# Second attention of a fused attention and MLP kernel: six more exps summed by VectorE, two new instruction orders, and batch 2's statistics moved behind it

## The chip, the cores and the metric

One core of one Trainium2 chip runs the whole program. The time is the device time of one execution in microseconds, the median of several runs. TensorE (PE in the profile) multiplies matrices, VectorE (DVE), ScalarE (ACT) and GpSimd (POOL) work on elements, and SyncE (SP) issues most of the transfers. The engines run side by side, each through its own queue in order, and wait for each other by semaphores. The matmul memory PSUM is used here as eight banks of 512 float32 columns.

## The reference

Attention with normalised queries and keys, then a two-layer MLP:

```python
q_n, k_n = rmsnorm(q, g_q), rmsnorm(k, g_k)        # x / sqrt(mean(x * x) + 1e-6) * g
attn = softmax(q_n @ k_n.T / 8)                    # 8 batches, 12 heads, 448 x 448
x = concat_heads(attn @ v)                         # 3584 x 768
out = gelu_tanh(x @ w_in) @ w_out                  # 768 -> 2048 -> 768
```

Inputs and output are float32; the matmuls run in bfloat16.

## The kernel before, in words

The batches are worked one after another, and two stages overlap. `attention(b)` does the attention of batch b and, in its gaps, the second MLP layer of the batch before. Behind it stands the first MLP layer of batch b, in whose time the operands of batch b + 1 are prepared. The attention of batch 0 has its own code; "the second attention" is that of batch 1.

**The twelve heads** go in three groups of four, called c = 0, 1, 2; group 1 holds "the middle heads". A group has seven units. A unit (line 335) is four 64x64 matmuls of scores into a pair of PSUM banks; ScalarE takes the exp of it (line 343) into SBUF. When a group's seven exps are there, TensorE sums them for the softmax (word `s`) and multiplies them with v (word `x`), both in `products` (line 387), which issues four matmuls for each operand in its list `es`. To shorten the sum, VectorE can add exps beforehand: step A adds exps 0, 1 to 2, 3 (line 355), B adds 4, 5 (line 358), F folds the two halves into one (line 360), G adds exp 6 (line 362). `added(b, c)` says how many are added; in the second attention it gives 6, 0 and 5 for the three groups. After the sum come T (two transposes, line 397), R (reciprocal, line 402), S (spread, line 409), and M (line 422), which writes `xT`, the input of the first layer.

**The order** of the attention is written out by hand. In `SECOND` (line 577) the first string is TensorE's order (`5r` is five steps of four matmuls of the second layer, line 495; `u` a unit), the second is VectorE's, and the third says before which exp ScalarE copies a finished tile of the second layer out. Words such as `J0`, `K0`, `L0`, `a0` in VectorE's string are places for further work, given to them in a list `extra`.

**PSUM** is four pairs of banks in a ring (`rounds`); `pair(...)` takes the one that was taken longest ago. The second layer holds one during the attention. In the first layer, `mm1_turn(b, i, ...)` works on the i-th of eight pairs of tiles, in turns: the first three pairs begin with the first two thirds of the sum ("early") before the loop over f, since the last `xT` isn't there yet. At f = 1 and f = 3 the "late" thirds of pairs 0 and 1 follow, at f = 5 that of pair 2, which also opens pair 3. When a pair is complete, ScalarE applies the Gelu (line 543).

**The preparation of batch 2:** for each group, squares of q and k (line 164 on GpSimd, line 162 on ScalarE), their totals over 64 columns (line 173, VectorE), a root, the product with the root (line 278, GpSimd), a transpose by DMA (line 319, SyncE), and for k a gain (line 325, VectorE). Groups 0 and 1 have their squares and totals at the places J0 to a5 of the second attention and their roots from ScalarE's Ln and Exp at its end. Group 2's squares follow at the end of the attention; its totals and its root by Newton's method (`rsqrt_last`, lines 254 to 262, 14 VectorE instructions) are issued at f = 0 of batch 1's first layer. Newton keeps two of its operands in PSUM, in a pair of their own from `pair("root")`.

Of the kernel before, what the change touches and what calls it, by code (L numbers as in the profile page):

```python
# [17 lines left out]
def kernel(  # L18
# [11 lines left out]
    nc = tc.nc  # L30
    B, H, S, D = q.shape
# [38 lines left out]
    def pair(name):  # L70
        rounds.append(rounds.pop(0))
        return rounds[-1]
# [65 lines left out]
    def late_loads(b, c):  # L138

        for n in "qk":  # L140
            for go in load(b, c, n):
                nc.vector.memset(raws[n, b, c][:1, 0, 0, :1], 0.0)
                go()
# [13 lines left out]
    def square(b, c, n, eng, hs=both, ts=slice(0, NT)):  # L157
        if (n, b, c) not in sqs:
            sqs[n, b, c] = sqp.tile([P, 2, NT, D], F32, tag="sq", name="sq")
        sq, raw = squares(b, c, n, hs, ts), raws[n, b, c][:, hs, ts]  # L160
        if eng is nc.scalar:
            nc.scalar.activation(sq, raw, AF.Square)  # L162
        else:
            eng.tensor_mul(sq, raw, raw)  # L164
# [5 lines left out]
    def total(b, c, n, hs=both, ts=slice(0, NT)):  # L170
        if b not in sss:
            sss[b] = smp.tile([P, NCH, 2, 2, NT], F32, tag="ss", name="ss")
        nc.vector.reduce_sum(  # L173
            sss[b][:, seat(b, c), "qk".index(n), hs, ts], squares(b, c, n, hs, ts), axis=AX.X
        )
# [6 lines left out]
    def place(b, c):  # L182
        if (b, c) == (0, NCH - 1):
            t = ps_m.tile([128, 512], F32, tag="mm", name="root")[:, :4 * NT]
        else:
            i = c % 2 * 4 * NT
            t = oall[1][:, S + i:S + i + 4 * NT]
        roots["qk", b, c] = t.rearrange("p (n a t) -> p n a t", n=2, a=2)
        for n in range(2):
            roots.setdefault(("qk"[n], b, c), roots["qk", b, c][:, n])  # L190
        return t
# [48 lines left out]
                dst, t[:, js], 1.5, y[:, js], op0=ALU.add, op1=ALU.mult  # L240
            )

    def rsqrt_last(b):


        c, flat, m = slice(NCH - 1, NCH), "p c n a t -> p (c n a t)", 4 * NT
        y, ms = rinvs[b][:, c].rearrange(flat), sss[b][:, c].rearrange(flat)
        if steady():
            own, dst = pair("root")[:, 0], y
        else:  # L250
            own, dst = oall[0][:, S:], place(b, 1)
        z, u = own[:, :m], own[:, m:2 * m]
        t = smp.tile([P, NCH * 4 * NT], F32, tag="lg", name="lg")[:, :m]
        nc.vector.tensor_scalar(u, ms, 1.0 / D, 1e-6, op0=ALU.mult, op1=ALU.add)
        nc.vector.tensor_scalar(
            y.bitcast(I32), u.bitcast(I32), -0.5, float(0x5F3759DF), op0=ALU.mult, op1=ALU.add
        )
        for i in range(3):
            nc.vector.tensor_copy(z, y)
            nc.vector.tensor_mul(t, z, y)  # L260
            nc.vector.scalar_tensor_tensor(z, t, -0.5, u, op0=ALU.mult, op1=ALU.mult)
            nc.vector.scalar_tensor_tensor(
                y if i < 2 else dst, z, 1.5, y, op0=ALU.add, op1=ALU.mult
            )
# [81 lines left out]

    def added(b, c):

        return NT - 1 if b > 1 else (NT - 1, 0, NT - 2)[c] if b else 0

    def add_exps(b, c, step):
        ex = exs[b, c]
# [18 lines left out]
    def products(b, c, what, lo=0, hi=NT):  # L371

        if lo == 0 and steady():
            o = oas["o", c, what] = pair("o")
            oas[what] = oas[c, what] = [o[:, r, :S] for r in range(2)]
        elif lo == 0:
            oas[what] = spare.pop() if spare else [o[:, :S] for o in oall]
        o = oas[what]
        es = [exs[b, c][:, t] for t in range(NT)]
        if not what and added(b, c):  # L380
            es[:added(b, c) + 1] = [ess[b, c][:, 0]]
        n = len(es)
        for i in range(lo, min(hi, n)):
            for r in range(2):
                rs = slice(r * R, (r + 1) * R)
                for a in range(2):
                    nc.tensor.matmul(  # L387
                        o[r][a * D:(a + 1) * D],
                        vb[b % 2][rs, 2 * c + a, i] if what else ones[rs], es[i][rs, a],
                        start=(i == 0), stop=(i == n - 1),  # L390
                    )
# [156 lines left out]
    def mm1_pair(i, cs=range(HP), b=0, js=range(2)):  # L548
# [27 lines left out]
    )  # L576
    SECOND = (
        "3r u 5r uu 8r u 8r uu 8r u 5r u 4r u 7r us 4r u 4r u 3r uu 4r x 1r usu 3r u 6r u 2r u 5r"
        " uu 10r x 6r sx",
        "A0 L0 B0 F0 G0 J0 T0 R0 K0 S0 a0 a1 M0 T1 R1 S1 a2 A2 a3 B2 F2 M1 a4 a5 T2 R2 S2 M2",  # L580
        {6: 0, 14: 1, 21: 2},
    )

    def attention(b, side, extra, ends):
# [65 lines left out]
        for word in order.split():  # L650
            if word.endswith("r"):
                for _ in range(int(word[:-1])):
                    next(m2)
                    go_on()
                continue
            for w in word:
                k = n[w]
                n[w] += 1
                if w == "u":
                    for fn in side.get(k, ()):  # L660
                        fn()
                    unit(b, *units[k])
                    made.add(("unit", k))
                else:
                    last = added(b, k)
                    assert {("u", t) for t in range(k * NT, (k + 1) * NT)} <= made
                    assert w == "x" or not last or ("FG"[last - NT + 2], k) in made
                    products(b, k, "sx".index(w))
                    made.add((w, k))
                go_on()  # L670
# [254 lines left out]
    for b in range(B):  # L925
        m1, side, extra, ends = [], [], [], []
        if b == 0:

            m1 = [(0, lambda: total(1, 0, "k"),
                   lambda: total(1, 2, "q"), lambda: total(1, 2, "k"),  # L930
                   lambda: rsqrt_newton(1), lambda: normed_both(1, 2, nc.gpsimd),
                   lambda: normed(1, 0, "k", nc.gpsimd)),
                  (2, lambda: total(1, 1, "q"), lambda: total(1, 1, "k"),
                   lambda: normed(1, 0, "q", nc.vector), lambda: rsqrt_last(1),
                   lambda: normed_both(1, 1, nc.vector)),
                  (6, lambda: trans(1, 0, nc.scalar)),
                  (7, lambda: trans(1, 1))]
            extra += [("first", lambda: late_loads(2, 0)), ("L0", lambda: late_transposed(1, 2)),
                      ("L0", lambda: late_loads(2, 1)), ("a1", lambda: late_loads(2, 2)),
                      ("K0", lambda: gain(1, 2))]  # L940

            for n in "qk":
                sqs[n, 2, 1] = [
                    nrmp.tile([P, NT, 2, D], BF16, tag=f"nrm{m}", name="sq")
                    .rearrange("p t a d -> p (t a d)").bitcast(F32)
                    .rearrange("p (a t d) -> p a t d", a=1, t=NT) for m in "qk"
                ]

            extra += [("J0", lambda: gpsimd_waits(ess[1, 0][:1, 0, 0, :1])),
                      ("K0", lambda: gpsimd_waits(kT[:1, 2, 0, 0, :1]))]  # L950
            at = 0
            for c in range(2):
                for n in "qk":
                    for hs in (slice(0, 1), slice(1, 2)) if c else (both,):
                        extra += [
                            ("K0" if at else "J0",
                             lambda c=c, n=n, hs=hs: square(2, c, n, nc.gpsimd, hs)),
                            (f"a{at}", lambda c=c, n=n, hs=hs: total(2, c, n, hs))]
                        at += 1
        elif b + 1 < B:  # L960

            m1.append((0, lambda: gpsimd_waits(ess[b, NCH - 1][:1, 0, 0, :1])))
            for c in range(NCH):
                if b == 1 and c + 1 == NCH:
                    m1 += [(0, lambda: total(2, 2, "q")), (0, lambda: total(2, 2, "k")),
                           (0, lambda: rsqrt_last(2))]
                m1 += [(0, lambda c=c: normed_both(b + 1, c, nc.gpsimd)),
                       (4 * c + 4, lambda c=c: transposed(b + 1, c))]
            m1 += [(9, lambda: gain(b + 1, 0)), (14, lambda: gain(b + 1, 1))]
        if 0 < b and b + 2 < B:  # L970
            m1 += [(4, lambda: loads(b + 2, 1)), (8, lambda: loads(b + 2, 2))]
            for c, at in ((0, 4), (1, 9)):
# [38 lines left out]
            break  # L1011
        nc.scalar.preload_act_table_set(EXP_SET)
        if b + 2 < B:
            ends.append(lambda: rsqrt(b + 2, slice(0, NCH if b else NCH - 1)))
            side += [(0 if b else 11, lambda: load_v(b + 2, 0, HP))]
            if b + 3 < B:
                side.append((3, lambda: loads(b + 3, 0)) if b else (14, lambda: late_loads(3, 0)))
# [38 lines left out]
```

## Time and profile before

| what | us |
|---|---|
| median of 3 runs (391.13 to 391.48) | 391.18 |
| the profiled execution | 391.23 |
| its span, first to last instruction | 389.2 |
| second attention, TensorE's part | 50.07 to 75.93 |
| first layer of batch 1 | 75.93 to 94.54 |
| third attention | 94.54 to 121.38 |

Line numbers (L387) are those of the kernel before. In a view by groups, the figures behind the bar are the busy time and the mean of one instruction in ns, then the engine's idle time before the group and what ended it. In a timeline a row is its start, its length, the engine, the line, the operation, output and inputs, and how often it stands there in a row; a bracket gives the idle time ahead of it. In the chain of work that ended last, a row is the start, the length, the engine, the tile and the line. The table of windows gives each engine's busy time, the granted clock of TensorE, the share of the transfer engines and their GB/s. The ends of matmuls are modelled, so their starts are read.

### The profile page before, as it was taken

How to read it: one execution, taken by the hardware profiler on the slowest of the kernel's cores; microseconds unless marked ns; L12 is line 12 of the kernel's file. 1: busy time of each engine (PE TensorE's matmuls, PEld its weight loads, DVE VectorE, ACT ScalarE, POOL GpSimd, SP SyncE). 2: the span in 40 equal slices, each digit the busy share in tenths (PEclk: the TensorE clock that was granted, in tenths of full speed). 3: DMA queues.
4: the chain of work that ended last, by engine and by line, in shares of the span. 5: the costliest groups of instructions: out<-in, count | busy, mean ns of one | idle time of the engine just before them, and what ended most of it. 6: DMA issues, size and time to landing. Idle time of an engine off the chain costs nothing.

```text
span 389.2 us, 17542 instructions
## 1 busy us (share of the span) xinstructions
PE 380.6 (98%) x8060; PEld 294.0 (76%) x8060; DVE 235.9 (61%) x366; ACT 278.7 (72%) x353; POOL 126.3 (32%) x110
## 2 busy tenths in 40 slices
PE   7899999999999999999999999999999999999996
PEld 4565577877887788877888788877888778887664
DVE  5998938976596359836589257953598204980010
ACT  6995499767994689757995589946897449944300
POOL 5996506384005440093103740064300900000000
PEclk9999999999999999999999999999999999999999
DMA  8999999999614992379822995159631721120033
GB/s 266 322 231 211 210 230 263 223 200 264 113 44 100 243 213 58 80 132 217 194 65 65 214 227 103 45 110 251 108 80 50 125 44 42 44 65 4 2 83 81
DMA packets 64446, 54.68 MB, mean 141 GB/s; under 512 B 37620, under 2 KB 60020, under 8 KB 64372
## 3 DMA queue, kind: packets, MB, share of 16 engines
q1 hardware_dynamic: 53936, 41.33, 43.8%
q0 software_dynamic: 10128, 11.80, 18.5%
q8 instruction: 63, 1.03, 1.1%
q10 hardware_dynamic: 308, 0.43, 0.4%
q14 instruction: 11, 0.09, 0.1%
HBM read 45.61 MB, written 11.01 MB: 146 GB/s over the span
## 4 chain that ended last, share of the span: by engine, by line
PE 92%; ACT 5%; DMA 1%; issue 1%; DVE 0%; POOL 0%; DVEq 0%
PE t L537 33%; PE t L495 32%; PE t L387 9%; PE t L335 7%; PE t L463 5%; ACT ex L343 4%; PE t L556 4%; DMA rawq<-in_q_dram 1%; PE h L436 1%; PE tp L296 1%; PE o L387 0%; POOL nrmq L278 0%; ACT g L543 0%; DVE ss L173 0%; ACT sq L162 0%
## 5 line engine op out<-in xcount | busy, mean ns | idle before, releaser
L343 ACT ACTIVATE ex<-t,shift 128x896 bf16<-128x896 f32 x168 | 156.2, 1016 | 1.9 <-PE t L335 1.6
L495 PE MATMUL t<-wout,g 64*64 64x384 bf16 (+1 forms) x3456 | 150.6, 305 | 0.0
L537 PE MATMUL t<-xT,win 64*64 64x448 bf16 x2688 | 128.7, 349 | 0.3 <-ACT g L543 0.3
L495 PEld LDWEIGHTS <-g 64*64 64x64 bf16 x3456 | 112.9, 107 | 19.2
L537 PEld LDWEIGHTS <-win 64*64 64x64 bf16 x2688 | 96.6, 107 | 31.0 <-issue 0.5
L543 ACT ACTIVATE g<-t 128x896 bf16<-128x896 f32 x56 | 50.5, 915 | 57.1 <-PE t L537 57.1
L173 DVE TENSOR_REDUCE ss<-sq 128x14 f32<-128x896 f32 (+3 forms) x45 | 44.5, 997 | 51.9 <-ACT sq L162 49.1
L335 PE MATMUL t<-qT,kT 64*64 64x448 bf16 x672 | 58.2, 351 | 1.4 <-ACT ex L343 0.6
L799 POOL COPY mark<-es 1x1 bf16<-1x1 bf16 x7 | 1.2, 177 | 132.0 <-DVE es L362 128.3
L355 DVE TENSOR_TENSOR es<-ex 128x1792 bf16<-128x1792 bf16 x20 | 21.2, 1061 | 33.0 <-ACT ex L343 33.0
L278 POOL TENSOR_TENSOR nrmq<-rawq,rinv 128x896 bf16<-128x896 f32 (+1 forms) x21 | 34.9, 1660 | 18.6 <-ACT rinv L205 11.0
L278 POOL TENSOR_TENSOR nrmk<-rawk,rinv 128x896 bf16<-128x896 f32 (+1 forms) x21 | 34.4, 1640 | 0.0
L387 PE MATMUL t<-ex,vb 64*64 64x448 bf16 x588 | 31.9, 350 | 0.0
L335 PEld LDWEIGHTS <-kT 64*64 64x64 bf16 x672 | 25.5, 106 | 7.3 <-DVE kT L305 1.2
L397 DVE STREAM_TRANSPOSE st<-t 128x448 f32<-128x448 f32 x42 | 24.7, 626 | 9.7 <-PE t L387 9.7
L387 PEld LDWEIGHTS <-vb 64*64 64x64 bf16 x672 | 23.5, 107 | 7.3 <-issue 1.0
L409 DVE STREAM_TRANSPOSE rb<-rc 128x896 f32<-128x896 f32 (+1 forms) x25 | 26.7, 1068 | 0.3
L705 DVE COPY osb<-t 128x384 f32<-128x384 f32 (+1 forms) x4 | 2.0, 507 | 35.2 <-PE t L463 35.2
L422 DVE TENSOR_TENSOR xT<-t,rb 128x896 bf16<-128x896 f32 x21 | 22.8, 1087 | 0.8
L164 POOL TENSOR_TENSOR sq<-rawq 128x896 f32<-128x896 f32 (+1 forms) x9 | 13.6, 1513 | 28.6 <-DVE ss L173 27.3
L513 ACT COPY osb<-t 128x768 f32<-128x768 f32 (+1 forms) x18 | 12.6, 701 | 13.9 <-PE t L495 13.9
L358 DVE TENSOR_TENSOR es<-es,ex 128x1792 bf16<-128x1792 bf16 x20 | 21.3, 1063 | 0.7 <-ACT ex L343 0.6
(103 smaller groups left out, 313.5 us busy)
## 6 DMA issues: line engine op xcount, KB each, us to landing
rawq<-in_q_dram SPq DMA_DIRECT2D x22, 448.0 KB, 5.0
rawk<-in_k_dram SPq DMA_DIRECT2D x22, 448.0 KB, 5.8
out_dram<-osb SPq DMA_DIRECT2D x42, 192.0 KB, 2.7
vb<-in_v_dram POOLq DMA_DIRECT2D x6, 672.0 KB, 7.3
win<-in_moe_w_in_dram POOLq DMA_DIRECT2D x8, 384.0 KB, 10.8
wout<-in_moe_w_out_dram POOLq DMA_DIRECT2D x3, 768.0 KB, 17.1
out_dram<-osb SPq DMA_DIRECT2D x24, 96.0 KB, 3.7
vb<-in_v_dram POOLq DMA_DIRECT2D x2, 448.0 KB, 15.5
```

Source lines behind the costliest of these rows:

```text
L173: nc.vector.reduce_sum(sss[b][:, seat(b, c), "qk".index(n), hs, ts], squares(b, c, n, hs, ts), axis=AX.X)
L278: eng.tensor_mul(nrms[n, b, c][:, ts].rearrange("p t a d -> p a t d"), raws[n, b, c][:, :, ts], root[:, :, ts].to_broadcast([P, 2, m, D]),)
L335: nc.tensor.matmul(sc[r * R:(r + 1) * R, a, :S], kT[rs, c, t, r], qT[b][rs, c, :, r], start=True, stop=True,)
L343: nc.scalar.activation(exs[b, c][:, t], scs.pop((b, c, t))[:, :, :S], AF.Exp, scale=scale, bias=shift)
L358: nc.vector.tensor_add(es, es, ex[:, 4:6])
L387: nc.tensor.matmul(o[r][a * D:(a + 1) * D], vb[b % 2][rs, 2 * c + a, i] if what else ones[rs], es[i][rs, a], start=(i == 0), stop=(i == n ...
L397: nc.vector.transpose(st[:, r].rearrange("p a b -> p (a b)"), o[r])
L409: nc.vector.transpose(oas["rb"][:, rs].rearrange("p r s -> p (r s)"), rc.to_broadcast([128, (rs.stop - rs.start) * m, 32]),)
L422: nc.vector.tensor_mul(xT[b][:, 2 * c:2 * c + 2], oas["o", c, 1][:, :, :S], oas["rb"])
L495: mm = nc.tensor.matmul(o[a * R:(a + 1) * R, bank, :hi - lo], g[rs, f, at:at + R], wout[rs, f, lo:hi], start=(n == 0), stop=(n == len(step ...
L537: mm = nc.tensor.matmul(h[a * R:(a + 1) * R, j, :S], win[rs, c, at:at + R], xT[b][rs, c], start=begin and c == cs[0], stop=end and c == cs ...
L543: nc.scalar.activation(g[:, 2 * i:2 * i + 2, (b % 2) * S:(b % 2 + 1) * S], h[:, :, :S], AF.Gelu_apprx_tanh,)
```

## The change

1. `added(1, 1)` becomes 5: the middle heads' exps 0 to 5 are added by steps A and B. F isn't done for them: `products` takes the two added halves and exp 6, three operands instead of seven.
2. `SECOND` gets a new order for TensorE and for VectorE and other places for ScalarE's copies. Only two places a0 and a1 are left for totals, those of group 0.
3. Batch 2's group 1: the four half squares on GpSimd and the four half totals on VectorE go to f = 0 of batch 1's first layer, ahead of the totals of group 2. Its root leaves ScalarE's Ln and Exp and joins Newton, which now works on 56 columns and comes before all of GpSimd's products of batch 2 in the program.
4. Newton's two PSUM operands no longer take a pair of their own. They lie in columns 448 on of the two banks of the pair taken last, `rounds[-1]`.
5. The gain of batch 2's group 1 moves from f = 14 to the start of the third attention; the loads of batch 2's group 2 are issued at a0 instead of a1.

```diff
-    def rsqrt_last(b):
+    def rsqrt_last(b, c=slice(NCH - 1, NCH)):
...
         if steady():
-            own, dst = pair("root")[:, 0], y
+            z, u = (rounds[-1][:, i, S:S + m] for i in range(2))
+            dst = y
...
-        return NT - 1 if b > 1 else (NT - 1, 0, NT - 2)[c] if b else 0
+        return NT - 1 if b > 1 else (NT - 1, NT - 2, NT - 2)[c] if b else 0
...
-            es[:added(b, c) + 1] = [ess[b, c][:, 0]]
+            es[:added(b, c) + 1] = [ess[b, c][:, i] for i in range(1 + ((b, c) == (1, 1)))]
...
-        "3r u 5r uu 8r u 8r uu 8r u 5r u 4r u 7r us 4r u 4r u 3r uu 4r x 1r usu 3r u 6r u 2r u 5r"
-        " uu 10r x 6r sx",
-        "A0 L0 B0 F0 G0 J0 T0 R0 K0 S0 a0 a1 M0 T1 R1 S1 a2 A2 a3 B2 F2 M1 a4 a5 T2 R2 S2 M2",
-        {6: 0, 14: 1, 21: 2},
+        "7r u 1r uu 9r u 7r u 1r u 1r u 9r u 10r u 3r u 1r s 3r u 4r u 1r u 7r ux 2r u 3r u 4r us"
+        " 2r u 5r uu 4r u 2r x 10r sx",
+        "A0 L0 B0 F0 G0 J0 T0 R0 K0 A1 S0 B1 M0 a0 T1 R1 A2 S1 B2 F2 M1 a1 T2 R2 S2 M2",
+        {8: 0, 13: 1, 21: 2},
...
+            if b == 1:
+                halves = [(n, slice(a, a + 1)) for n in "qk" for a in range(2)]
+                m1 += [(0, lambda n=n, hs=hs: square(2, 1, n, nc.gpsimd, hs)) for n, hs in halves]
+                m1 += [(0, lambda n=n, hs=hs: total(2, 1, n, hs)) for n, hs in halves]
+                m1 += [(0, lambda n=n: total(2, 2, n)) for n in "qk"]
+                m1.append((0, lambda: rsqrt_last(2, slice(1, NCH))))
             for c in range(NCH):
-                if b == 1 and c + 1 == NCH:
-                    m1 += [(0, lambda: total(2, 2, "q")), (0, lambda: total(2, 2, "k")),
-                           (0, lambda: rsqrt_last(2))]
                 m1 += [(0, lambda c=c: normed_both(b + 1, c, nc.gpsimd)),
                        (4 * c + 4, lambda c=c: transposed(b + 1, c))]
...
-            ends.append(lambda: rsqrt(b + 2, slice(0, NCH if b else NCH - 1)))
+            ends.append(lambda: rsqrt(b + 2, slice(0, NCH if b else 1)))
```

More of the change, by code (lines that the diff above doesn't have):

```diff
@@ L241, in rsqrt_newton @@
             )
-    def rsqrt_last(b):
-        c, flat, m = slice(NCH - 1, NCH), "p c n a t -> p (c n a t)", 4 * NT
+    def rsqrt_last(b, c=slice(NCH - 1, NCH)):
+        flat, m = "p c n a t -> p (c n a t)", (c.stop - c.start) * 4 * NT
         y, ms = rinvs[b][:, c].rearrange(flat), sss[b][:, c].rearrange(flat)
         if steady():
-            own, dst = pair("root")[:, 0], y
-        else:
-            own, dst = oall[0][:, S:], place(b, 1)
-        z, u = own[:, :m], own[:, m:2 * m]
+            z, u = (rounds[-1][:, i, S:S + m] for i in range(2))
+            dst = y
+        else:
+            z, u = oall[0][:, S:S + m], oall[0][:, S + m:S + 2 * m]
+            dst = place(b, 1)
         t = smp.tile([P, NCH * 4 * NT], F32, tag="lg", name="lg")[:, :m]
@@ L666, in attention @@
                     assert {("u", t) for t in range(k * NT, (k + 1) * NT)} <= made
-                    assert w == "x" or not last or ("FG"[last - NT + 2], k) in made
+                    assert w == "x" or not last or ("BG" if (b, k) == (1, 1) else "FG")[
+                        last - NT + 2] + str(k) in {x + str(i) for x, i in made}
                     products(b, k, "sx".index(w))
@@ L938 @@
             extra += [("first", lambda: late_loads(2, 0)), ("L0", lambda: late_transposed(1, 2)),
-                      ("L0", lambda: late_loads(2, 1)), ("a1", lambda: late_loads(2, 2)),
+                      ("L0", lambda: late_loads(2, 1)), ("a0", lambda: late_loads(2, 2)),
                       ("K0", lambda: gain(1, 2))]
@@ L950 @@
                       ("K0", lambda: gpsimd_waits(kT[:1, 2, 0, 0, :1]))]
[L951 to L959, printed above, removed]
+            for at, n in enumerate("qk"):
+                extra += [
+                    ("JK"[at] + "0", lambda n=n: square(2, 0, n, nc.gpsimd)),
+                    (f"a{at}", lambda n=n: total(2, 0, n))]
         elif b + 1 < B:
             m1.append((0, lambda: gpsimd_waits(ess[b, NCH - 1][:1, 0, 0, :1])))
+            if b == 1:
[4 more added lines that the diff above has]
+                m1.append((0, lambda: rsqrt_last(2, slice(1, NCH))))
             for c in range(NCH):
-                if b == 1 and c + 1 == NCH:
-                    m1 += [(0, lambda: total(2, 2, "q")), (0, lambda: total(2, 2, "k")),
-                           (0, lambda: rsqrt_last(2))]
                 m1 += [(0, lambda c=c: normed_both(b + 1, c, nc.gpsimd)),
                        (4 * c + 4, lambda c=c: transposed(b + 1, c))]
-            m1 += [(9, lambda: gain(b + 1, 0)), (14, lambda: gain(b + 1, 1))]
+            m1.append((9, lambda: gain(b + 1, 0)))
+            if b == 1:
+                extra.append(("first", lambda: gain(2, 1)))
+            else:
+                m1.append((14, lambda: gain(b + 1, 1)))
         if 0 < b and b + 2 < B:
```

## The prediction

> **What bounds the kernel now.** First the stages in one table (the view of busy time by window), then the chain that ended last, then the VectorE timeline between the second attention and batch 1's first layer. The columns after the window are its length and each engine's busy time.
>
> ```profile
> core 0: us, PE busy (x) PEld busy (x) DVE busy (x) ACT busy (x) POOL busy (x), PEclk, DMA share, GB/s
> 50.07:75.93 25.86, 25.86 (x597) 19.54 (x601) 19.19 (x38) 23.48 (x31) 8.23 (x10) 1.00 0.95 238
> 75.93:94.54 18.61, 18.35 (x390) 13.76 (x385) 13.38 (x28) 13.05 (x19) 12.49 (x8) 1.00 1.14 221
> 121.38:139.54 18.16, 18.16 (x390) 13.84 (x385) 7.82 (x9) 10.88 (x16) 12.31 (x8) 1.00 0.94 199
> ```
>
> TensorE is busy throughout the second attention (first row) and all but 0.26 us of batch 1's first layer (second row); the same layer of batch 2 (third row) takes 0.45 us less. So a TensorE instruction removed here is worth its issue time, and any new wait of TensorE is paid in full. The chain shows the issue times, and one wait:
>
> ```profile
> 63.39 1.39 PE t L387 x28
> 65.13 1.44 PE t L387 x28
> 70.31 1.62 PE t L495 x40
> 71.93 1.32 PE t L387 x28
> 81.65 0.93 ACT g L543
> 82.62 11.92 PE t L537 x248
> 121.38 18.16 PE t L537 x384
> ```
>
> Four 64x64 matmuls run side by side, so 384 are 96 groups and one group takes 18.16/96 = 0.189 us; 28 in 1.32 us say the same. The 1.39 and 1.44 us pieces hold short waits for exps. At 81.65 TensorE waits for a Gelu: Newton's "root" holds one of the four PSUM pairs, so the layer's fourth tile pair must take the one that the first Gelu is still reading.
>
> **The change part by part.**
>
> *Fewer matmuls.* The totals of head group 1 of batch 1 (line 387) were seven groups over plain exps. Two adds leave three groups (two added rows and exp 6): four groups less, 4 x 0.189 = **-0.76 us**. The adds are two VectorE instructions (lines 355 and 358 measure 1.061 and 1.063 us), in place of four half totals that leave this attention.
>
> *New orders.* ScalarE gives its exps back to back:
>
> ```profile
> 51.55 5.50 ACT L343 ACTIVATE ex<-t,shift 128x896 bf16<-128x896 f32 x6
> ```
>
> Six in 5.50 us, the last one 1.02 long, are 0.90 apart. I laid the new word list out by hand with this step, the issue times above (a second-layer step of four matmuls 0.162 us: 40 in 1.62) and three PSUM pairs in turn, each free at the end of its exp; the old list laid out so ends within 0.03 us of the trace. The new one holds TensorE up for 0.3 to 0.4 us in all, as the old one does: taken as 0, ends -0.3 and +0.3. TensorE then reaches the first layer at 75.73 - 0.76 = 75.0.
>
> *The PSUM pair set free.* The wait ahead of 82.62 goes, and the layer's 18.61 us become batch 2's 18.16: **-0.45 us**. ScalarE's Ln and Exp at the end cover 28 columns instead of 56, under 0.1 us beside TensorE work: 0.
>
> *The totals of batch 2's middle heads, behind the attention.* They move from VectorE's queue in the attention to behind its last step, in front of Newton, and Newton now does 56 columns.
>
> ```profile
> 72.61 0.62 DVE L360 TENSOR_TENSOR es<-es 128x896 bf16<-128x896 bf16 x1
> 73.30 1.09 DVE L422 TENSOR_TENSOR xT<-t,rb 128x896 bf16<-128x896 f32 x1
> 74.31 1.14 DVE L173 TENSOR_REDUCE ss<-sq 128x7 f32<-128x448 f32 x2
> 75.36 1.17 DVE L397 STREAM_TRANSPOSE st<-t 128x448 f32<-128x448 f32 x2
> 78.17 1.09 DVE L422 TENSOR_TENSOR xT<-t,rb 128x896 bf16<-128x896 f32 x1
> 79.18 2.07 DVE L173 TENSOR_REDUCE ss<-sq 128x14 f32<-128x896 f32 x2
> 81.28 0.19 DVE L254 TENSOR_SCALAR t<-ss 128x28 f32<-128x28 f32 x1
> 84.19 0.18 DVE L262 SCALAR_TENSOR_TENSOR rinv<-t,rinv 128x28 f32<-128x28 f32 x1
> 73.37 0.18 POOL L799 COPY mark<-es 1x1 bf16<-1x1 bf16 x1 [3.70 <-DVE es L360]
> 67.01 1.83 POOL L164 TENSOR_TENSOR sq<-rawk 128x448 f32<-128x448 f32 x2
> 37.58 0.22 DVE L233 SCALAR_TENSOR_TENSOR lg<-lg,ss 128x56 f32<-128x56 f32 x1
> 37.83 0.22 DVE L235 SCALAR_TENSOR_TENSOR rinv<-lg,rinv 128x56 f32<-128x56 f32 x1
> ```
>
> The last add (72.61) follows the last exps, which ScalarE gives back to back in both orders: I keep its time to 0.2 us. Behind it one whole total replaces two halves, so the last xT product still starts near 78.0 and ends near 79.0. Then come four half totals, 4 x 0.53 = 2.1 us, and the two whole ones, 2.1 us: Newton starts near 83.2 instead of 81.28. GpSimd's four half squares, 0.92 us each behind the mark at 73.37, are done at 77.2 and hold nobody up. The loads of batch 2's last heads go out one step sooner, with two VectorE marks of 0.06 us: 0, as nothing waits for them before 77. Newton's 14 instructions stand 0.224 us apart with 28 columns and 0.25 apart with 56 (37.58 to 37.83): 14 x 0.25 less the two shorter first steps is 3.4 us, so it ends near **86.6**, ends 86.2 and 87.1.
>
> *Newton's operands in unused columns.* They lie behind column 448 of both banks of the last pair taken, that of the third tile pair of the first layer (`hs1[2]`). TensorE has written its early part there and comes back at f = 5. Whether that is a wait, this row and the next one say:
>
> ```profile
> L837 PE MATMUL t<-gbf,rows 32*128 32x32 bf16 x2 | 0.2, 184 | 1.8 <-DVE nrmq L278 1.8
> 75.73 6.63 PE L537 MATMUL t<-xT,win 64*64 64x448 bf16 x136
> ```
>
> Line 837 writes columns 0 to 31 of `gall`. The VectorE product that it waited 1.8 us for reads only columns 448 on of the same bank, and shares nothing else with it. So a matmul is ordered behind an earlier VectorE access of the same bank, whatever the columns. I take it so here. The layer's 33rd group is the first of f = 5: before, it started at 75.73 + 32 x 0.189 = 81.78; after, TensorE is there at 75.0 + 6.05 = 81.1 and stands until 86.65, **5.6 us**. Behind the waiting matmul stand all the later groups, and behind these ScalarE's Gelus. Nothing covers it. What the matmuls save is swallowed, since Newton's end and no longer TensorE sets the time: 86.65 - 81.78 - 0.45 = **+4.4 us**; ends +4.0 and +4.9.
>
> [...]
>
> *The clock after such a wait.* No wait of TensorE as long as this is in the trace. The bounds are these two answers for the same matmul, before 3.3 us and from 3.6 to 6.0 us, and the mean behind line 837's 1.8 us:
>
> ```profile
> L269 PE MATMUL o<-const-bfloat16-1.0 128*128 128x256 bf16 x13 | 2.9, 414 | 0.8 <-PEq L1040 0.8
> L269 PE MATMUL o<-const-bfloat16-1.0 128*128 128x256 bf16 x16 | 2.1, 280 | 0.0
> L296 PE MATMUL tp<-ident,nrmq 128*128 128x128 bf16 x35 | 3.0, 220 | 0.1
> ```
>
> From rest, 13 matmuls took 0.22 us each and later ones 0.13: a slow restart of that length costs 13 x 0.09 = 1.2 us. After 1.8 us there is no sign of one. So 0 to 1.2; 5.6 us is nearer to rest than to 1.8, and I take **+0.8**.
>
> [...]
>
> *What stands later on the queues.* GpSimd's products of heads 1 and 2, SyncE's two pairs of transposes and batch 3's loads between them, GpSimd's last squares, VectorE's totals and gains at the start of the third attention: all hang on Newton and come some 2.3 to 4 us later. With TensorE itself 4.4 us late they are hidden: 0. The moved gain is 0.44 us of VectorE there, also ahead of need.
>
> **Sum:** -0.76 and -0.45 are inside the +4.4; with the clock +5.2. From the profiled execution's 391.23 (span 389.2 and about 2 around it) 396.4; the median 391.18, 0.05 lower, gives **396.4** too.
>
> **The rivals.**
>
> *No wait on Newton (ordered by columns).* Then the queues just named decide, in the third attention:
>
> ```profile
> 84.50 1.69 POOL L278 TENSOR_TENSOR nrmq<-rawq,rinv 128x896 bf16<-128x896 f32 x1 [1.68 <-issue]
> kT<-nrmk SPq DMA_TRANSPOSE x3, 5.8
> 96.55 0.44 DVE L325 TENSOR_SCALAR kT<-kT,gcols 128x896 bf16<-128x896 bf16 x1
> 100.56 1.09 DVE L355 TENSOR_TENSOR es<-ex 128x1792 bf16<-128x1792 bf16 x1 [3.56 <-ACT ex L343]
> 101.57 0.95 DVE L513 COPY osb<-t 128x768 f32<-128x768 f32 x1
> ```
>
> GpSimd's four products start at 86.75 and end at 93.4; the last transpose goes out near 94.4 and lands 5.8 to 6.1 us later, near 100.4; the gain takes 0.44, and the third attention's first add starts at 100.8, where TensorE, 1.2 us early, would want it at 99.4. The copy behind it frees a PSUM pair for a unit at once, so TensorE waits 1.4 us and the kernel is 0.2 us slower than before: **391.4**, no change. For it: the columns are disjoint. Against it: line 837.
>
> *No wait, and the later transfers land in time.* Faster: -0.76 - 0.45 = -1.2, **390.0**. It ends there if that last gain is over by 99.4, 1.4 us sooner than worked out; the 3.56 us for which VectorE idled before its add speak for it, the landing times against.
>
> *Newton longer still.* If GpSimd's squares come over 1.9 us late, each further us delays Newton by as much: 397 and more, slower too, in the range.
>
> **How the numbers follow.** Wait for Newton, with its clock term: 0.91. No wait, no change: 0.05. No wait, faster: 0.04. A measurement of this kernel can tell about 0.2% (0.8 us) from no change, so slower 0.91, same 0.05, faster 0.04. The range is the forecast's own: 395.2 (+4.0, full clock) to 397.9 (+4.9, 1.2 of slow restart, and 0.6 for a restart beyond what the start shows). The rivals outside hold 0.09.
>
> **What would show it.** Right: line 537 idle about 5.6 us before its 33rd group, ended by VectorE line 262; no wait for a Gelu behind it; 108 instead of 124 matmuls of line 387 in the second attention; line 269's slow rate again in the groups behind the wait, or not. Wrong: line 537 unbroken and the wait in the third attention instead; or Newton's end away from 86.6, whose error goes into the time one for one.

## The result, and the profile after

The changed kernel takes **398.19 us** (median of four runs, 397.89 to 399.09) where the kernel before takes 391.16 beside it: ratio 1.018, 95% interval 1.0163 to 1.0200. The prediction was 396.4 us with a range of 395.2 to 397.9. The direction and the mechanism are as forecast; the time lies 0.3 us above the range. The profiled execution of after took 397.89 us with a span of 396.1, 6.66 us above the one of before (391.23).

First the TensorE timeline of the changed kernel around batch 1's first layer, then the layer's line in the page's list of the costliest groups, then the 33rd group seen in the chain that ended last.

```profile
75.45 6.25 PE L537 MATMUL t<-xT,win 64*64 64x448 bf16 x128
87.01 13.25 PE L537 MATMUL t<-xT,win 64*64 64x448 bf16 x236 [5.30 <-DVE rinv L262]
```

```profile
L537 PE MATMUL t<-xT,win 64*64 64x448 bf16 x2688 | 130.6, 352 | 5.3 <-DVE rinv L262 5.3
```

```profile
86.74 0.23 DVE rinv L262
86.97 0.04 issue
87.01 14.22 PE t L537 x193
```

The 128 matmuls from 75.45 are the 32 groups ahead of the first "late" part of pair 2. The 33rd group stands for 5.30 us, and what releases it is Newton's last VectorE instruction. No Gelu is named behind it: the pair that "root" took is free, and its 0.26 us wait is gone. Across the whole kernel this is the only wait of line 537.

The queues that feed this moment, VectorE first and then GpSimd:

```profile
62.38 1.09 DVE L355 TENSOR_TENSOR es<-ex 128x1792 bf16<-128x1792 bf16 x1
64.42 1.68 DVE L358 TENSOR_TENSOR es<-es,ex 128x1792 bf16<-128x1792 bf16 x1
66.02 1.08 DVE L422 TENSOR_TENSOR xT<-t,rb 128x896 bf16<-128x896 f32 x1
78.17 1.09 DVE L422 TENSOR_TENSOR xT<-t,rb 128x896 bf16<-128x896 f32 x1
79.18 4.17 DVE L173 TENSOR_REDUCE ss<-sq 128x7 f32<-128x448 f32 x6
83.46 0.22 DVE L254 TENSOR_SCALAR t<-ss 128x56 f32<-128x56 f32 x1
...
86.49 0.22 DVE L261 SCALAR_TENSOR_TENSOR t<-lg,t 128x56 f32<-128x56 f32 x1
86.74 0.21 DVE L262 SCALAR_TENSOR_TENSOR rinv<-t,rinv 128x56 f32<-128x56 f32 x1
```

```profile
62.50 1.01 POOL L800 COPY mark<-kT 1x1 bf16<-1x1 bf16 x1 [1.03 <-DVE kT L325]
63.47 1.67 POOL L164 TENSOR_TENSOR sq<-rawk 128x896 f32<-128x896 f32 x1
87.09 1.69 POOL L278 TENSOR_TENSOR nrmq<-rawq,rinv 128x896 bf16<-128x896 f32 x1 [6.13 <-DVE rinv L262]
```

The six totals stand as laid out, 79.18 to 83.35; Newton starts at 83.46 and ends at 86.95. In the attention, the middle heads' new step B (64.42) is 1.68 us long, where the prediction took the mean of 1.06.

Now busy times by window, with TensorE's granted clock in the third column from the end. The first row is the whole second attention; the others are the time around the wait in pieces of 3.41 us:

```profile
core 0: us, PE busy (x) PEld busy (x) DVE busy (x) ACT busy (x) POOL busy (x), PEclk, DMA share, GB/s
50.09:75.45 25.36, 25.10 (x576) 18.52 (x580) 19.05 (x35) 23.12 (x29) 6.86 (x8) 1.00 1.00 241
80.66:84.07 3.41, 1.04 (x24) 0.59 (x17) 3.23 (x7) 2.19 (x3) 0.30 (x1) 1.00 0.82 145
84.07:87.48 3.41, 0.47 (x8) 0.33 (x11) 2.51 (x12) 0.00 (x0) 0.39 (x1) 0.50 0.72 255
87.48:90.89 3.41, 3.41 (x44) 2.11 (x40) 0.00 (x0) 0.00 (x0) 3.41 (x3) 0.50 0.28 53
90.89:94.30 3.41, 3.41 (x80) 2.45 (x75) 1.23 (x2) 3.12 (x5) 2.83 (x2) 1.00 1.04 95
```

The clock changes at 84.07 and at 90.89; the other edges of the four short windows lie half of that stretch, 3.41 us, from these. TensorE runs out of work at 81.7; at 84.07 the granted clock falls to 0.50 and stays there until 90.89, for 6.82 us. Some 2.9 us of that lie under the wait, but from 87.01 to 90.89 TensorE works at half rate: 44 matmuls in the row from 87.48, where the next one, at full clock, holds 80.

**The sum of the profiled execution.** The 33rd group starts at 87.01 instead of 81.78 (+5.23); the Gelu wait behind it is gone and the rest of the layer is 0.45 shorter, so +4.8. From there the chain has 14.22 us to the end of the layer, where before they were 12.76 (81.78 to 94.54), less the 0.45 12.31: the slow clock costs **1.9 us**. Together 6.7: TensorE comes to the third attention at 101.01 instead of 94.35. In that attention 0.3 more is lost (batch 2's first layer begins at 128.13 instead of 121.19, +6.94), so the span is 6.9 us longer; the two times differ by 6.66.

### The profile page after: what moved, and what is told of

It is laid out like the page before. It is cut to its first block, busy times and chain, and to the rows that moved or that the text cites. A ratio compares the mean times of both kernels' runs of the same rounds, so it can differ in the third digit from the quotient of the medians.

```text
span 396.1 us, 17513 instructions
## 1 busy us (share of the span) xinstructions
PE 383.1 (97%) x8044; PEld 292.5 (74%) x8044; DVE 240.9 (61%) x368; ACT 278.9 (70%) x353; POOL 127.2 (32%) x110
## 3 DMA queue, kind: packets, MB, share of 16 engines
q8 instruction: 63, 1.03, 1.1%
## 4 chain that ended last, share of the span: by engine, by line
PE 81%; ACT 8%; DVE 7%; issue 2%; DMA 1%; POOL 0%; DVEq 0%
PE t L537 31%; PE t L495 26%; ACT ex L343 7%; PE t L387 7%; PE t L335 6%; PE t L463 5%; PE t L556 4%; DVE ss L173 2%; DVE st L397 1%; DMA rawq<-in_q_dram 1%; DVE xT L422 1%; DVE es L358 1%; PE h L436 1%; DVE es L355 1%; PE tp L296 0%
## 5 line engine op out<-in xcount | busy, mean ns | idle before, releaser
L537 PE MATMUL t<-xT,win 64*64 64x448 bf16 x2688 | 130.6, 352 | 5.3 <-DVE rinv L262 5.3
L495 PEld LDWEIGHTS <-g 64*64 64x64 bf16 x3456 | 111.6, 107 | 20.7 <-PE t L495 0.3
L355 DVE TENSOR_TENSOR es<-ex 128x1792 bf16<-128x1792 bf16 x21 | 22.3, 1062 | 32.4 <-ACT ex L343 32.4
L358 DVE TENSOR_TENSOR es<-es,ex 128x1792 bf16<-128x1792 bf16 x21 | 22.9, 1091 | 0.6 <-ACT ex L343 0.6
```

The lines of the kernel that those rows point to most:

```text
L358: nc.vector.tensor_add(es, es, ex[:, 4:6])
L495: mm = nc.tensor.matmul(o[a * R:(a + 1) * R, bank, :hi - lo], g[rs, f, at:at + R], wout[rs, f, lo:hi], start=(n == 0), stop=(n == len(step ...
L537: mm = nc.tensor.matmul(h[a * R:(a + 1) * R, j, :S], win[rs, c, at:at + R], xT[b][rs, c], start=begin and c == cs[0], stop=end and c == cs ...
```

## The experiments

Line numbers in kernels with added lines are one to three higher than those of before. Each time stands beside runs of the kernel before on the same chip. The theory throughout: the operands in the pair's unused columns make the 33rd group wait for Newton (about 4.7 us), and the clock that falls during the wait costs the rest.

**e1_own_pair** takes back the operands' place alone:

```diff
-            z, u = (rounds[-1][:, i, S:S + m] for i in range(2))
+            own = pair("root")[:, 0]
+            z, u = own[:, :m], own[:, m:2 * m]
```

> The changed kernel with Newton's two operands back in a PSUM pair of their own; all else as changed. Theory (the 5.7 us wait comes from sharing the bank with TensorE, and the slow matmuls behind it from that wait): line 537 isn't held by VectorE any more, Newton still ends near 87.0, and what is left is the later queue of transposes, loads and totals: the third attention's first add at 101.4 to 101.8 instead of 100.56, so 391.9 to 392.4. Rival (the 7 us come from the totals and the longer Newton behind the attention, wherever the operands lie): 397 to 398.

Measured: **391.65 us**, ratio 1.0017 (1.0003 to 1.0031). TensorE's timeline, and VectorE's at the start of the third attention:

```profile
82.18 11.92 PE L538 MATMUL t<-xT,win 64*64 64x448 bf16 x248 [0.26 <-ACT g L544]
102.75 0.38 PE L336 MATMUL t<-qT,kT 64*64 64x448 bf16 x4 [0.33 <-DVE osb L514]
```

```profile
100.37 0.46 DVE L326 TENSOR_SCALAR kT<-kT,gcols 128x896 bf16<-128x896 bf16 x1 [0.33 <-DMA kT<-nrmk]
100.74 1.09 DVE L356 TENSOR_TENSOR es<-ex 128x1792 bf16<-128x1792 bf16 x1
```

The wait for VectorE is gone and the Gelu wait of before is back. 6.5 us of the 7.0 hang on where two small operands lie. What the matmuls saved is lost again in the third attention, which takes 0.5 us longer in this trace (93.91 to 121.29, before 94.35 to 121.19). There batch 2's last gain and so the first add come late: the place and the time that the prediction gave its first rival (add at 100.8), earlier than the 101.4 to 101.8 expected of this run, whose time is below the expected 391.9 too. The profiled execution is the fastest of the twelve, 391.02. TensorE's wait for the copy behind it is shorter than the rival's, 0.33 us against 1.4, as TensorE came only 0.44 early (93.91 against 94.35 for the first second-layer matmul) and not 1.2.

**e3_columns_only** does that one part alone, in the kernel before: Newton's operands (28 columns) in the unused columns, everything else untouched.

```diff
-            own, dst = pair("root")[:, 0], y
+            z, u = (rounds[-1][:, i, S:S + m] for i in range(2))
+            dst = y
...
```

> The kernel before with nothing changed but the place of Newton's two operands: columns 448 on of the pair taken last. Theory (ordered by bank): Newton ends near 84.4 and line 537's 33rd group, due at 81.8, waits 2.6 us for it; less the 0.45 us of the Gelu wait 393.4 at full clock, and up to 3 us more in executions where the clock falls. Rival (disjoint columns are free, the changed kernel's wait has another cause): 390.7.

Measured: **394.97 us**, ratio 1.0081 (1.0061 to 1.0101). The six runs are of two kinds: 393.21 twice, and 394.94 to 395.19 four times. The profiled execution is one of the second kind (394.94):

```profile
84.45 13.98 PE L538 MATMUL t<-xT,win 64*64 64x448 bf16 x256 [2.52 <-DVE rinv L263]
```

```profile
81.00:84.40 3.40, 0.93 (x20) 0.49 (x13) 2.84 (x15) 2.19 (x3) 1.76 (x2) 1.00 0.91 203
84.40:87.80 3.40, 3.35 (x40) 2.25 (x43) 0.00 (x0) 0.00 (x0) 3.27 (x2) 0.56 1.20 297
87.80:91.20 3.40, 3.40 (x72) 2.57 (x68) 1.09 (x1) 3.05 (x5) 0.07 (x1) 0.94 1.17 282
```

A wait of 2.52 us, and a mean clock of 0.56 in the 3.4 us behind it. The two kinds lie 1.8 us apart, about half of those 3.4 us. That 393.21 is the same wait with the clock held is inferred. The mean granted clock of the runs fits it, 0.998 and 1.000 in the two of 393.21 and 0.994 to 0.996 in the four others, but no trace of the quicker kind is there.

**e4_fillers** leaves the wait as it is and gives TensorE 27 matmuls of constants to do in it, into a pair that is free then; they compute nothing that is used.

```diff
                 m1.append((0, lambda: rsqrt_last(2, slice(1, NCH))))
+                m1.append((4, lambda: idle(27, rounds[0][:, 0])))
```

> The changed kernel with 27 extra matmuls of 448 columns (about 5.1 us, their results unused) just ahead of the 33rd group, so that TensorE is busy while it would wait. Theory (1.9 to 3.1 us of the loss are a slow restart after the idle stretch): the granted clock stays at 1.0, groups behind Newton's end stand 0.189 us apart at once, 395.8 to 396.1. Rival (the restart costs something else, such as the refilling of the pipeline): 398 as without them.

Measured: **395.88 us** (395.79 to 396.09), ratio 1.0119 (1.0105 to 1.0132).

```profile
81.45 5.36 PE L269 MATMUL t<-const-bfloat16-1.0 128*128 128x448 bf16 x27
86.83 12.30 PE L537 MATMUL t<-xT,win 64*64 64x448 bf16 x256
```

Line 537 now goes on 0.02 us behind the fillers and at full rate at once (granted clock 1.00 from 86.83 to 90.24): 256 matmuls in 12.30 us, where the chain of after has 14.22 for the same 64 groups. This splits the loss in two. The wait itself costs 395.88 - 391.16 = **4.7 us**; the clock costs 398.19 - 395.88 = **2.3 us**, and 2.0 to 3.2 by the single runs of after.

**e7_square_later** concerns the attention. GpSimd's second square of batch 2's first group moves behind the middle heads' step B:

```diff
-                      ("K0", lambda: gpsimd_waits(kT[:1, 2, 0, 0, :1]))]
+                      ("a0", lambda: gpsimd_waits(ess[1, 1][:1, 0, 0, :1]))]
...
-                    ("JK"[at] + "0", lambda n=n: square(2, 0, n, nc.gpsimd)),
+                    (("J0", "a0")[at], lambda n=n: square(2, 0, n, nc.gpsimd)),
```

> The changed kernel with one GpSimd instruction moved: the square of batch 2's k, group 0, waits until VectorE's step B of the middle heads is done. Theory (in the changed attention that step took 1.68 us instead of 1.06 because it shares its operands' path with GpSimd's square, and the unit behind it waited 0.45 us): the step takes 1.06 to 1.10 us, the first layer begins 0.3 to 0.45 us earlier, and the time doesn't move, 397.9 to 399.1, since Newton's end sets it. Rival (the step is long for another reason, or TensorE's hold has another cause): step and start of the first layer as in the changed kernel.

Measured: **398.55 us**, ratio 1.0168 (1.0146 to 1.0191). VectorE's step B, TensorE's wait, and the attention as one window:

```profile
64.86 1.04 DVE L358 TENSOR_TENSOR es<-es,ex 128x1792 bf16<-128x1792 bf16 x1
```

```profile
87.14 13.06 PE L537 MATMUL t<-xT,win 64*64 64x448 bf16 x224 [5.49 <-DVE rinv L262]
```

```profile
50.49:75.40 24.91, 24.91 (x576) 18.46 (x580) 18.34 (x34) 22.82 (x29) 5.87 (x8) 1.00 1.04 262
```

With GpSimd out of the way step B takes 1.04 us, TensorE is busy for the whole 24.91 us, and the attention, 25.66 us in before and 25.36 in after, is 0.75 shorter: the 0.76 of the four groups. The first layer begins only 0.05 earlier than in after, at 75.40, and not the 0.3 to 0.45 expected, since in this execution the attention began 0.40 later (50.49 instead of 50.09). The time doesn't move, as expected: Newton's end (87.14 for the 33rd group) still sets it.

The other five look for what is left of the change once the operands lie elsewhere.

**e6_sbuf** is the kernel before with Newton's operands in SBUF, so that no pair is taken and no bank is shared:

```diff
-            own, dst = pair("root")[:, 0], y
+            z, u = (
+                smp.tile([P, NCH * 4 * NT], F32, tag="lg", name=n)[:, :m] for n in ("nz", "nu")
+            )
+            dst = y
...
```

> The kernel before with Newton's two operands in SBUF, so that neither a pair is taken nor a bank shared. Theory (the pair kept by Newton costs 0.45 us in batch 1's first layer): the Gelu wait goes, 390.7, if Newton, which now runs beside GpSimd's products with two SBUF inputs, ends less than 1 us later. Rival (the wait moves to another place, or the contention holds the transposes up): 391.2 or more.

Measured: 391.22 us (390.14 to 394.42), ratio 1.0002 (0.9985 to 1.0020): a miss, no gain that can be told. The profiled execution is the slowest of the twelve, with a mean granted clock of 0.991 where the others have 0.998 to 1.000; its times stand about 3 us late (the second attention begins at 52.80 instead of 50.07) and only durations are read. TensorE, VectorE and GpSimd:

```profile
81.46 16.46 PE L540 MATMUL t<-xT,win 64*64 64x448 bf16 x343 [0.66 <-issue]
```

```profile
84.27 1.57 DVE L257 TENSOR_SCALAR nu<-ss 128x28 f32<-128x28 f32 x1
```

```profile
84.12 1.68 POOL L281 TENSOR_TENSOR nrmk<-rawk,rinv 128x896 bf16<-128x896 f32 x1
```

No Gelu wait is left. But Newton's first instruction, 0.19 us long on PSUM, takes 1.57 beside a GpSimd product, and TensorE waits 0.66 us for something that the trace doesn't name. Newton being later costs nothing in this execution, as the third attention's first add still idles 3.56 us for its exps; the 0.66 us make the layer 19.08 us long to the first second-layer matmul instead of 18.62. Two more traces here have such a stop of TensorE, which the chain of work calls "issue": 0.44 us in e10_total_at_z0 and 0.81 in e11_total_at_z1. What they are, and so where the 0.45 us went in the other runs, stays open.

**e8_sbuf_late_gain** is the changed kernel with the operands in SBUF as in e6_sbuf, and batch 2's last gain behind the first add of the third attention (a place Z0 behind G0 in VectorE's order) instead of ahead of it:

```diff
-        "A0 E0 B0 F0 G0 T0 R0 A1 S0 B1 F1 M0 G1 T1 R1 A2 S1 B2 F2 G2 M1 T2 R2 S2 M2",
+        "A0 E0 B0 F0 G0 Z0 T0 R0 A1 S0 B1 F1 M0 G1 T1 R1 A2 S1 B2 F2 G2 M1 T2 R2 S2 M2",
...
-            extra.append(("first", lambda: gain(b + 1, 2)))
+            extra.append(("Z0" if b == 1 else "first", lambda: gain(b + 1, 2)))
```

> The changed kernel with Newton's operands in SBUF and the gain of batch 2's group 2 behind step G of the third attention's first group instead of ahead of its first add. Theory (without the shared bank the queue of transposes, loads and totals decides, and of it the gain's transpose landed last): no wait of line 537 for VectorE or for a Gelu, the third attention's first add at 99.9 to 100.2, 390.5 to 390.8. Rival (the totals of batch 3 in front of that add hold it just as long): 391.3 to 391.7, as with the pair of its own.

Measured: 391.36 us, ratio 0.9996 (0.9979 to 1.0013): again no gain. TensorE once, then VectorE:

```profile
68.62 0.38 PE L337 MATMUL t<-qT,kT 64*64 64x448 bf16 x4 [1.81 <-DVE rawk L142]
```

```profile
63.49 0.45 DVE L327 TENSOR_SCALAR kT<-kT,gcols 128x896 bf16<-128x896 bf16 x1 [1.46 <-DMA kT<-nrmk]
...
65.89 1.68 DVE L360 TENSOR_TENSOR es<-es,ex 128x1792 bf16<-128x1792 bf16 x1
...
100.58 1.09 DVE L173 TENSOR_REDUCE ss<-sq 128x14 f32<-128x896 f32 x1 [0.55 <-POOL sq L164]
101.58 1.08 DVE L357 TENSOR_TENSOR es<-ex 128x1792 bf16<-128x1792 bf16 x1
```

Two things ate it. In the new attention the middle heads' adds stand on VectorE behind a gain that waits for a transpose; in this execution that landed late, the gain waited 1.46 us, step B was 1.68 us long again, and TensorE waited 1.81. And in the third attention the first add now stands behind batch 3's last total, which waits for GpSimd's square: with the gain gone, the totals hold it, as the rival had it.

**e9_both** joins the edits of e8_sbuf_late_gain and e7_square_later.

> The edits of the two other kernels of this call together. Theory: TensorE comes to the third attention 0.3 to 0.45 us earlier than without the moved square and waits there for the same add, so 390.5 to 390.8 again, not less. Rival (TensorE's arrival and not VectorE's queue decides): 390.1 to 390.4.

Measured: 391.00 us, ratio 0.9983 (0.9968 to 0.9998). TensorE, then VectorE:

```profile
102.72 0.38 PE L337 MATMUL t<-qT,kT 64*64 64x448 bf16 x4 [1.03 <-DVE osb L515]
```

```profile
98.08 1.09 DVE L173 TENSOR_REDUCE ss<-sq 128x14 f32<-128x896 f32 x1 [4.09 <-POOL sq L164]
99.71 1.09 DVE L173 TENSOR_REDUCE ss<-sq 128x14 f32<-128x896 f32 x1 [0.55 <-POOL sq L164]
100.72 1.08 DVE L357 TENSOR_TENSOR es<-ex 128x1792 bf16<-128x1792 bf16 x1
```

The third attention starts at 93.10 instead of 94.35, and its first add waits behind the same total; TensorE gives 1.03 us back there. The time is above what both the theory (390.5 to 390.8) and the rival (390.1 to 390.4) had, and the interval ends just below 1.

**e10_total_at_z0** and **e11_total_at_z1** move that total too, behind the attention's first G (Z0) or its second (Z1). The edit to e9_both, for Z1:

```diff
-        "A0 E0 B0 F0 G0 Z0 T0 R0 A1 S0 B1 F1 M0 G1 T1 R1 A2 S1 B2 F2 G2 M1 T2 R2 S2 M2",
+        "A0 E0 B0 F0 G0 Z0 T0 R0 A1 S0 B1 F1 M0 G1 Z1 T1 R1 A2 S1 B2 F2 G2 M1 T2 R2 S2 M2",
...
-                extra.append(("first", lambda n=n: total(b + 2, 2, n)))
+                extra.append(("Z1" if (b, n) == (1, "k") else "first", lambda n=n: total(b + 2, 2, n)))
```

> The kernel of e9_both with one more step of VectorE moved: the last total of batch 3 (that of its keys' last group, 1.09 us for each of its two halves or so) no longer stands ahead of the third attention's first add, but behind that attention's first G, beside the gain that e9_both has there. In e9_both the first add started at 100.72, held by those totals, and TensorE waited 1.03 us for the copy behind it. Theory (the totals in front of the first add hold the attention by about 1 us): the first add starts near 99.3, as soon as its four exps are there, TensorE's wait for the copy at 102.7 shrinks below 0.3 us, and the time is 390.0 to 390.4. Rival (VectorE's queue in the third attention is full, and the moved total delays the transposes and sums behind it as much as it helped the add): the wait moves to a later unit or sum, and the time is 391.0 or more.

> As e10_total_at_z0, with that total behind the second G of the third attention instead of the first, where fewer units hang on VectorE. Theory (only the place ahead of the first add was wrong): first add near 99.3, no wait of TensorE for VectorE above 0.3 us in the attention's first half, time 390.0 to 390.4, equal to or below e10_total_at_z0. Rival (VectorE's queue is full throughout the third attention, or the root of batch 3, which needs this total, comes late): 391.0 or more, with the wait later than in e10_total_at_z0.

Measured: Z0 390.73 us, ratio 0.9989 (0.9976 to 1.0002); Z1 **390.36 us** (389.79 to 391.14), ratio 0.9965 (0.9948 to 0.9982), the one furthest below before. TensorE at Z0, then at Z1:

```profile
107.02 0.38 PE L337 MATMUL t<-qT,kT 64*64 64x448 bf16 x4 [0.32 <-DVE st L399]
```

```profile
101.54 0.38 PE L337 MATMUL t<-qT,kT 64*64 64x448 bf16 x4 [0.16 <-DVE osb L515]
...
107.55 1.33 PE L497 MATMUL t<-wout,g 64*64 64x384 bf16 x28 [0.81 <-ACT ex L345]
```

VectorE at Z0, then at Z1:

```profile
100.17 1.09 DVE L357 TENSOR_TENSOR es<-ex 128x1792 bf16<-128x1792 bf16 x1 [1.20 <-ACT ex L345]
```

```profile
98.05 1.09 DVE L173 TENSOR_REDUCE ss<-sq 128x14 f32<-128x896 f32 x1 [3.88 <-POOL sq L164]
99.08 1.54 DVE L357 TENSOR_TENSOR es<-ex 128x1792 bf16<-128x1792 bf16 x1
```

In both the first add no longer stands behind the moved total. At Z0 it waits for its exps, and the wait is only handed on, to the transposes behind the total (0.32 us for line 399), as the rival had it; the time lies between the theory's 390.4 and the rival's 391.0. At Z1 the add starts right behind the total that is left ahead of it (98.05), 1.64 us sooner than in e9_both, and the wait for the copy is 0.16. The time is in the theory's 390.0 to 390.4. Not all fits: this profiled execution is the slowest of its eight runs (391.14), TensorE gives 0.81 us back at 107.55, and it reaches batch 2's first layer at 121.33, no sooner than before (121.19). The row names an exp for the 0.81 us, the chain of the same execution nothing ("issue"); whether the faster runs go without isn't shown.

## Why the prediction was right and wrong

**The wait, right.** Line 537 was to stand about 5.6 us before its 33rd group, released by VectorE's line 262; it stood 5.30. The net was to be +4.4 (4.0 to 4.9); by e4_fillers it is 4.7, by the profile 4.8. e1_own_pair (no wait of line 537 for VectorE) and e3_columns_only (2.52 us) show that the operands' place makes it, and so that the matmul is ordered here behind earlier VectorE accesses though the columns are disjoint. The prediction read this from the row of line 837 as an order by bank. The traces fit one that is coarser here: the 33rd group's first matmul writes the pair's second bank, which Newton reads last in line 261 (ended 86.71), yet it starts at 87.01, behind line 262, whose one PSUM operand lies in the first bank. Line 837 is the same case, as its first matmul writes the bank that the VectorE product doesn't read, and waits too (1.8 us). Order by bank and order by the whole pair aren't told apart by any run, as none puts the operands in one bank alone of a pair that TensorE comes back to; for the sum it is 0.3 us at most.

**Newton, slightly short.** Forecast to end near 86.6 (86.2 to 87.1), measured 86.95. It started at 83.46 instead of 83.2, and its first two instructions stand 0.25 us apart like the others, where I had let them be shorter. That is the 0.3 us between 4.4 and 4.7.

**The clock: the step that failed.** "From rest, 13 matmuls took 0.22 us each and later ones 0.13 ... So 0 to 1.2; 5.6 us is nearer to rest than to 1.8, and I take +0.8." It measured 1.9 us in the profiled execution and 2.3 in the medians, and with it the sum left the range: 4.7 + 2.3 = 7.0 against 5.2. The sign and the mechanism were right, the size was not; without the clock's loss (e4_fillers, 395.88) the time lies in the range. The 13 slow matmuls at line 269 were taken as the whole of a restart, so its upper bound was too low. What counted is the time from the restart to the return of the full clock: 87.01 to 90.89, 3.9 us at half rate, a loss of half of it. Two more traces agree. In e7_square_later TensorE is back at 87.14, and from there to the second layer it takes 14.38 us, 2.3 more than the 12.10 of e4_fillers; at half rate that is 4.6 us, up to about 91.7, an estimate, as of that trace only the mean clock of 0.990 stands here. In e3_columns_only the clock is 1.00 in the 3.4 us up to 84.40 and falls behind the restart at 84.45: the means of 0.56 and 0.94, taken as stretches at 0.50 and at 1.00, put it low from about 84.8 to 88.2, an estimate, and half of these 3.4 us is 1.7; the way to the second layer takes 13.78 us, 1.7 more. The single runs of after lost 2.0 to 3.2 us against e4_fillers, but only one of them has a trace, and their mean clocks are alike (0.990 to 0.991), so that their spread comes from the clock isn't shown. The forecast's range had 0.6 more at its upper end for a restart beyond what the start shows: no run shows that term by itself, and the three traces have 1.7 to 2.3 us for the whole.

**Fewer matmuls and the new order, half right.** 108 matmuls of line 387 instead of 124 are in the trace, but the attention was 0.30 us shorter and not 0.76. I had costed the order at 0 with VectorE's adds at their mean; the middle heads' step B (1.68 us) runs beside GpSimd's square, and a unit waits 0.26 us for what stands behind it. e7_square_later takes the square away and has the 0.75. None of it reached the end, since the wait sets the time, as forecast.

**The pair set free, right:** no Gelu wait, the rest of the layer 0.45 us shorter apart from the clock. **The later queues, right** as hidden in after, where the third attention's first add (107.22) is as late as TensorE, 6.66 us, and still idles 3.56 us for its exps; the 0.3 us lost in that attention behind the add were not in the prediction's sum. In e1_own_pair, where they aren't, the add is late as the first rival said, and the time is 391.65 against its 391.4. The rival of 390.0 needed a third attention whose first add comes on time; e11_total_at_z1, which puts the operands in SBUF and moves a gain, a square and a total on VectorE's and GpSimd's queues, comes to 390.36.

## What to carry to other kernels

Space that was free in a PSUM pair wasn't free of order here: operands put beside a tile that TensorE came back to tied it to their last use, for 4.7 us. When a wait of TensorE of some 2.5 us or more is in the forecast, add a term for the clock, and not a guess from the start of the kernel: the traces here lost 1.7 to 2.3 us behind waits of 2.52 to 5.49 us, about half of the time from the restart to the return of the full clock, and two of six runs with a wait of 2.5 us lost none, by their times. And a cut of 1.2 us in two neighbouring stages came to 0.9 us at the end (391.25 to 390.36) only after a square, a gain and a total had been moved as well: look for the next queue that will be late before counting a saving.

## What the runs showed of the hardware that wasn't expected

The clock fell at 84.07, 2.4 us after TensorE had run out of work; in the 3.41 us ahead of the fall it had still worked for 1.04. In e3_columns_only it fell after a wait of 2.52 us, in the profiled execution and, by the times and the mean clocks, in three of the five others. The two other runs (393.21 us, mean clocks 0.998 and 1.000) fit the same wait without the fall.

VectorE's add of two SBUF tensors took 1.68 us instead of 1.04 beside GpSimd's square of SBUF data. It started at 64.42, the square ended at 65.14, and the product behind the add started at 66.02; GpSimd's one-element copy at 62.50 took 1.01 instead of 0.18 us, to the end of VectorE's add that had begun at 62.38. The times fit an instruction that does its work only behind the other: 62.38 + 1.09 = 63.47, where the square starts, and 65.14 + 1.04 = 66.2, 0.1 us from the 66.1 at which the add ends. In e7_square_later, with the square behind the add, the two took 1.04 and 0.18 us. What of the two instructions makes the one wait for the other isn't shown.
